# Gated linear attention before a mixture of experts: holding every second sequence with its chunk halves exchanged, and leaving out the scores that the causal mask removes

## The chip, the cores and the metric

The kernel runs on one NeuronCore of a Trainium2 chip. The metric is the device time of one execution in microseconds (us). The engines are named as in the profile: PE is the matrix engine (PEld its weight loads), DVE the vector engine, ACT the scalar engine, POOL the GpSimd engine, and SP the engine that issues most of the DMAs.

## The reference, cut to what matters

An attention block with a decaying state feeds an expert layer with two levels of routing. There are 4 batches, 8 heads, 768 steps and a head size of 48; 3072 tokens of 384 features reach 16 experts with a hidden size of 1024.

```python
def _attn_ref(q, k, v, f_logit):                 # each (4, 8, 768, 48)
    f = 1.0 / (1.0 + np.exp(-f_logit))
    for t in range(S):
        state = f[:, :, t, :, None] * state + np.einsum('bhd,bhe->bhde', k[:, :, t], v[:, :, t])
        y[:, :, t] = np.einsum('bhd,bhde->bhe', q[:, :, t], state)

def _moe_ref(x, w_group, w_expert, w1, w2):      # x (3072, 384)
    # argmax of x @ w_group picks a group, argmax of xg @ w_expert[g] an expert in it
    h = np.maximum(xg[mask_e] @ w1[g, e], 0.0)
    out[tok_idx] = (g_w * e_w)[:, None] * (h @ w2[g, e])
```

## The kernel before

**The attention part** works on chunks of 128 steps. A unit is one chunk of two sequences (two batches, eight heads each), so there are 6 x 2 = 12 units, numbered 0 to 11; even and odd units are the two pairs of batches of the same chunk. In a unit the sequences are called b = 0 and 1, the eight heads are four pairs a with a member r = 0 or 1. A chunk's 128 steps lie on the 128 partitions as they come from memory; after a transpose the two heads of a pair lie on partitions 0 to 47 and 64 to 111.

A unit runs through stages, each a generator that issues a little of its work at each step:

- load (L568): four transfers on SP's queue, f, k, q and v, each of both sequences (f of unit 0 in two). k and q of unit i+2 and f of unit i+3 are asked for at the start of unit i.
- bounded, gated (L577, L584): the log gates, their cumulative sum over the chunk as a matmul with the triangle `tri` (L600), and two exponentials of it. The last row of one exponential goes by a small DMA to `ends` (L607); `decayed` (L638) turns it into the decay of the chunk.
- multiplied, turned (L614, L626): q and k times those exponentials on DVE (L620, L623), then transposes (L634) copied by ACT to Tq and Tk (L635).
- scored (L647): for every head the 128 x 128 products of keys and queries, written as two matmuls, one for each half of the keys, with all 128 queries (L659). DVE multiplies them by `tri` (L662), which leaves queries at or after their key. The result is `am`, one tile for each sequence.
- stated (L665): keys times values (L676) for the state of the next chunk (`sp`, `st`, L682 and L683 on DVE).
- weighed (L688): in its first step the state times the queries (L697, from the second chunk on), in its second the values times `am` (L701), both summed in the same two PSUM banks; ACT copies them to xT (L704).
- done, listed (L707, L729): logits of the router (L717), and rows of x turned back (L742) and sent to memory.

PSUM is eight banks given out in turn under the name bank. Matmuls with 48 rows and 64 columns use one of four tiles of the array, those of 128 rows and 64 columns one of two. Every fp32 product appears in the trace as two pairs of a weight load and a matmul; the transposes appear as one.

**The order of the work** on PE, DVE, ACT and SP is written out by hand: BEGIN for units 0 to 2, EVEN and ODD for the others, ORDERS for the last. A letter with an offset names the stage and the unit. In EVEN "s s s s c+2 w d-1 g+2 w" means: scores of b = 0, their masks, scores of b = 1, their masks, then the state products, the router logits of the unit before, and the outputs. POOL's order is left to the scheduler.

**The routing** of a chunk (route, L178) runs step by step among the units, mainly on DVE. After chunk 3 two experts are picked early and their weights loaded; after the last chunk all are ranked. **The expert part** runs 16 passes of two matmuls each (up L432 and L439, down L465 with L460 or L475), with tokens gathered and results scattered by indirect DMAs of POOL (L393, L450). Two early passes fill PE while the last routing runs. Behind the passes stand a slower path for gates that decay too far (scan) and one for experts with more tokens than foreseen; both are skipped with these inputs.

Of the kernel before, what the change touches and what calls it, by code (L numbers as in the profile page):

```python
# [10 lines left out]
FP32 = mybir.dt.float32  # L11
# [4 lines left out]
OP = mybir.AluOpType  # L16
AX = mybir.AxisListType.X
ET = mybir.EngineType
P = 128
# [4 lines left out]
def kernel(  # L24
# [12 lines left out]
    nc = tc.nc  # L37
# [56 lines left out]
    halves = const([P, 2], FP32, "halves")  # L94
    make_upper_triangular(nc, tri, val=1.0, diag=True)
    make_identity(nc, ident)
    nc.vector.memset(onesb, 1.0)
    nc.vector.tensor_tensor(strictb, tri, ident, OP.subtract)

# [219 lines left out]

    def choose(sb):  # L320
        number = numbers(sb)
        mine = sb.tile([P, 2, HP, P], FP32, tag="am", bufs=3, name="mine").rearrange("p r a t -> p (r a t)")[:, 0:2 * GE * GE].rearrange("p (n j e) -> p n j e", j=2, e=GE)
# [196 lines left out]
    with ExitStack() as fast:  # L519
# [44 lines left out]
        def parts(i):  # L564

            return (slice(0, 1), slice(1, 2)) if i == 0 else (slice(0, 2),)

        def load(i, names):  # L568
            c, s = units[i]
            w = live.setdefault(i, {"v": pads["v"][i % 4], "qh": pads["qh"][i % 3]})  # L570
            for nm in names:
                if nm not in w:
                    w[nm] = sb.tile([P, 2, H, D], FP32, tag="ld_" + nm, bufs=3 if nm == "f" else 2, name="ld_" + nm)
                for b in parts(i) if nm == "f" else (slice(0, 2),):
                    nc.sync.dma_start(out=heads(w[nm][:, b])[:, :, 0:D], in_=SRC[nm][2 * s + b.start:2 * s + b.stop, :, c * P:(c + 1) * P, :].rearrange("b h t d -> t (b h) d"))

        def bounded(i):  # L577

# [5 lines left out]
        def gated(i):  # L584

            c, s = units[i]
            w = live[i]

            nl = w["f"].rearrange("p b h d -> p b (h d)")
            for b in parts(i):  # L590
                nc.scalar.activation(nl[:, b], nl[:, b], AF.Exp, bias=0.0, scale=-1.0)
                if i:
                    yield
                nc.scalar.activation(nl[:, b], nl[:, b], AF.Ln, bias=1.0, scale=1.0)
            eq, qh, kh = pads["eq"][i % 2], w["qh"], pads["kh"][i % 3]
            w.update(eq=eq, kh=kh)
            yield
            for b in range(2):
                cs = bank([P, H, D], "cs")
                nc.tensor.matmul(cs.rearrange("t h d -> t (h d)"), lhsT=tri, rhs=nl[:, b], start=True, stop=True)  # L600
                nc.scalar.activation(eq[:, b, :, 0:D], cs, AF.Exp, bias=0.0, scale=-1.0)  # L601
                nc.scalar.activation(kh[:, b, :, 0:D], cs, AF.Exp, bias=0.0, scale=1.0)
                if b:

                    if s == 0:
                        ends[c] = sb.tile([B * HP, P], FP32, tag="ends", bufs=1, name="ends")
# [40 lines left out]
        def scored(i):  # L647
            w = live[i]
            w["am"] = []
            for b in range(2):  # L650
                am = sb.tile([P, 2, HP, P], FP32, tag="am", bufs=3, name="am")
                w["am"].append(am)
                ap = [bank([P, HP, P], f"ap{r}") for r in range(2)]
                for a in range(HP):
                    for r in range(2):
                        rows = slice(DP * r, DP * r + D)
                        for u in range(2):
                            half = slice(u * P // 2, (u + 1) * P // 2)
                            nc.tensor.matmul(ap[r][half, a, :], lhsT=w["Tk"][rows, b, a, half], rhs=w["Tq"][rows, b, a, :], start=True, stop=True)  # L659
                yield  # L660
                for r in range(2):
                    nc.vector.tensor_tensor(am[:, r], ap[r], tri.unsqueeze(1).broadcast_to((P, HP, P)), OP.mult)  # L662
                yield

        def stated(i):  # L665
# [22 lines left out]
        def weighed(i):  # L688
# [7 lines left out]
                        rows = slice(DP * (b ^ h), DP * (b ^ h) + D)  # L696
                        nc.tensor.matmul(ys[b][DP * h:DP * h + DP, a, :], lhsT=states[s][c % 2][rows, b, a, :], rhs=w["Tq"][rows, b, a, :], start=(a == 0), stop=False, skip_group_check=True)  # L697
            yield
            for b in range(2):
                for a, h in [(a, h) for a in range(HP) for h in range(2)]:  # L700
                    nc.tensor.matmul(ys[b][DP * h:DP * h + DP, a, :], lhsT=w["v"][:, b, 2 * a + (b ^ h), :], rhs=w["am"][b][:, b ^ h, a, :], start=(c == 0 and a == 0), stop=True, skip_group_check=True)  # L701
# [77 lines left out]
        def advance(gens):  # L779
# [8 lines left out]
        STAGES = {"c": bounded, "g": gated, "m": multiplied, "t": turned, "s": scored, "n": stated, "w": weighed, "d": done, "x": listed, "b": decayed}  # L788
        BEGIN = """c0 g0 p g0 g0 m0 m0 m0 m0 l2 t0 t0 t0 t0 h c1 g1 g1 s0 s0 s0 s0 g1 g1 p w0 w0 n0 m1 m1 m1 m1 l3 h x0 x0 x0
            t1 t1 t1 t1 b1 c2 g2 g2 s1 s1 s1 s1 p d0 g2 g2 n0 n1 w1 w1 m2 m2 l4 n1  # L790
            d0 x1 x1 t2 t2 t2 t2 c3 g3 g3 x1 s2 s2 s2 s2 w2 g3 g3 d1 w2 n2 m3 m3 c4 g4 g4""".split()
        BEGUN = 3
        EVEN = "l+2 d-2 n-1 r r r x-1 x-1 t t t t g+1 g+1 x-1 r s s s s c+2 w d-1 g+2 w g+2 n m+1 m+1".split()
        ODD = "l+2 d-2 r r x-1 x-1 t t t t b n-1 g+1 g+1 x-1 r s s s s c+2 w d-1 g+2 w g+2 n m+1 m+1 r n".split()
        ORDERS = {
            NU - 3: "l+2 o d-2 r r x-1 x-1 t t t t b n-1 r g+1 g+1 x-1 r s s s s c+2 w d-1 g+2 w g+2 n m+1 m+1 r n".split(),
            NU - 2: "d-2 r x-1 x-1 r t t t t r g+1 g+1 x-1 s s s s w d-1 w n m+1 m+1".split(),
            NU - 1: "d-2 r r n-1 x-1 x-1 t t t t r x-1 r s s s s w b d-1 w r r".split(),
            NU: "d-2 r e d-1 x-1 x-1 d-1 x-1 r r r e e r e r r e r r e r e r r e e e e e".split(),
        }  # L800
        steps_of = {}
# [144 lines left out]
    def scan():  # L946
# [42 lines left out]
        for c in range(NC):  # L989
            lgs = sb.tile([P, B, NL], FP32, tag="lgs2", name="lgs2")  # L990
            for b in range(B):
                x = sb.tile([P, HP, 2, DP], FP32, tag="x2", name="x2")
                nc.vector.memset(x, 0.0)
                for r in range(2):
                    nc.sync.dma_start(out=x[:, :, r, 0:D], in_=y_dram[b * HP:(b + 1) * HP, c * P:(c + 1) * P, r * D:(r + 1) * D].rearrange("a t d -> t a d"))
# [72 lines left out]
```

## Time and profile before

| What | Value |
|---|---|
| Median of 14 runs | 422.36 us (420.86 to 423.38) |
| Profiled execution | 421.6 us, of which the span is 419.7 us |
| PE busy | 408.8 us (97%), 4047 matmuls |
| PEld busy | 376.4 us (90%) |
| DVE, ACT, POOL busy | 266.8, 156.8 and 83.0 us |
| Scores L659 | 24.4 us on PE, x768 |
| Outputs L701 | 24.4 us on PE, x384 |
| State products L697, keys times values L676 | 10.7 and 11.0 us, x320 each |
| Masks L662 | 29.8 us on DVE, x48 |
| Attention part | to about 137 us of the span, then the expert passes |
| Mean granted clock of PE | 0.993 |

A busy figure counts the time in which at least one instruction of the group ran, so matmuls that lie side by side in the array count once; the mean of one is much longer than its share. A line of the form "start, length, what" in the chain of waits is a stretch of the work that ended last, in order of time; "x64" is the number of instructions in it. In the timeline, a bracket gives the idle time before the first of a group and what ended it.

### The profile page before, as it was taken

To read this page: it belongs to the slowest core of one execution; us is meant where nothing else is said; L and a number is where in the kernel's file an instruction comes from. 1 tells how busy PE (TensorE), PEld (TensorE's weight loads), DVE (VectorE), ACT (ScalarE), POOL (GpSimd) and SP (SyncE) were. 2 spreads that over 40 slices of the span, in tenths; PEclk is the share of its full clock that TensorE was granted. 3 is DMA by queue.
4 is the path that set the end of the run, shared out by engine and by line. 5 is a ranking of instruction groups with operands and counts; after the bars stand their busy time and mean duration, and the time that the engine had idled before them with its cause. 6 is when DMAs were issued, how large, how long until landed. Compare 5 with 4: busy or idle time off the path is not lost.

```text
span 419.7 us, 10066 instructions
## 1 busy us (share of the span) xinstructions
PE 408.8 (97%) x4047; PEld 376.4 (90%) x4047; DVE 266.8 (64%) x778; ACT 156.8 (37%) x353; POOL 83.0 (20%) x127
## 2 busy tenths in 40 slices
PE   7999999999999998999999999999999999999995
PEld 3888888888878966879999999999999999999992
DVE  5666878878897810550599786495595595594240
ACT  6777776667554311111123122231231231231220
POOL 4000010101012166001031321312222221120230
PEclk9999999999999999899999999999999999999998
DMA  9999997878999369937548485595695795585010
GB/s 176 197 202 215 188 179 152 155 141 157 334 340 387 110 242 340 372 120 278 177 154 291 121 313 199 199 328 134 249 318 141 276 301 197 216 319 161 27 46 24
DMA packets 132145, 88.98 MB, mean 212 GB/s; under 512 B 102582, under 2 KB 122748, under 8 KB 132090
## 3 DMA queue, kind: packets, MB, share of 16 engines
q1 hardware_dynamic: 125666, 75.50, 61.4%
q0 software_dynamic: 5792, 11.92, 9.4%
q10 hardware_dynamic: 632, 0.83, 0.6%
q8 instruction: 34, 0.56, 0.6%
q14 instruction: 21, 0.17, 0.1%
HBM read 78.71 MB, written 9.83 MB: 211 GB/s over the span
## 4 chain that ended last, share of the span: by engine, by line
PE 48%; issue 29%; DMA 8%; POOL 6%; DVE 4%; another core or an unknown queue 2%; POOLq 1%; ACT 1%; SPq 0%; DVEq 0%
PE hp L439 11%; DMA out_dram<-yt,xg 6%; PE yo L475 6%; PE ap L659 5%; PE y L701 5%; POOL out_dram L450 4%; PE cs L600 3%; PE yo L460 3%; PE x_ps L742 2%; POOL xg L393 2%; PE tr_k L634 2%; PE ds L676 2%; PE y L697 2%; PE tr_q L634 2%
## 5 line engine op out<-in xcount | busy, mean ns | idle before, releaser
L439 PE MATMUL hp<-xe,w 128*128 128x128 f32 (+14 forms) x864 | 141.7, 323 | 2.2 <-issue 1.5
L439 PEld LDWEIGHTS hp<-xe,w 128*128 128x128 f32 x864 | 137.5, 192 | 4.4 <-issue 2.4
L475 PE MATMUL yo<-h,w 128*128 128x230 f32 (+13 forms) x672 | 115.8, 333 | 0.0
L422 DVE STREAM_TRANSPOSE yr<-yT 32x192 f32<-32x192 f32 (+1 forms) x208 | 70.5, 339 | 70.5 <-ACT yT L476 67.9
L475 PEld LDWEIGHTS yo<-h,w 128*128 128x128 f32 x672 | 113.7, 190 | 0.2
L415 DVE STREAM_TRANSPOSE xe<-xg 32x192 f32<-32x192 f32 (+1 forms) x208 | 69.7, 335 | 8.7 <-PE hp L439 5.7
L440 ACT ACTIVATE h<-hp 128x256 f32<-128x256 f32 (+14 forms) x72 | 34.2, 478 | 109.1 <-PE hp L439 102.3
L450 POOL DMA_INDIRECT out_dram<-yt,xg x32 | 34.4, 1076 | 155.5 <-ACT yt L447 150.0
L476 ACT COPY yT<-yo 128x230 f32<-128x230 f32 (+13 forms) x42 | 13.5, 325 | 80.5 <-PE yo L475 80.5
L393 POOL DMA_INDIRECT xg<-x_dram,rows_p x30 | 29.6, 986 | 51.7 <-DMA out_dram<-yt,xg 29.1
L662 DVE TENSOR_TENSOR am<-ap,tri 128x512 f32<-128x512 f32 x48 | 29.8, 682 | 12.0 <-PE ap L659 12.0
L659 PE MATMUL ap<-Tq,Tk 48*64 48x128 f32 x768 | 24.4, 273 | 0.5 <-issue 0.5
L701 PE MATMUL y<-am,v 128*64 128x128 f32 x384 | 24.4, 276 | 0.2
L701 PEld LDWEIGHTS y<-am,v 128*64 128x64 f32 x384 | 20.9, 137 | 3.3 <-issue 1.8
L659 PEld LDWEIGHTS ap<-Tq,Tk 48*64 48x64 f32 x768 | 21.0, 133 | 2.5 <-issue 2.0
L460 PE MATMUL yo<-w,h 128*128 128x384 f32 x64 | 21.3, 486 | 0.0
L600 PE MATMUL cs<-ld_f,tri 128*128 128x384 f32 x48 | 18.6, 506 | 0.5 <-issue 0.4
L460 PEld LDWEIGHTS yo<-w,h 128*128 128x128 f32 x64 | 11.9, 190 | 7.4
L447 ACT ACTIVATE yt<-yr,xg 128x384 f32<-128x384 f32 (+13 forms) x26 | 14.4, 604 | 5.4 <-DVE yr L422 5.4
L607 POOL DMA_DIRECT2D ends<-eq x10 | 5.4, 541 | 55.7 <-ACT eq L601 55.7
L704 ACT COPY xT<-y 128x512 f32<-128x512 f32 x24 | 13.5, 580 | 4.4 <-PE y L701 4.3
L430 DVE COPY xe<-xg_ps 128x384 f32<-128x384 f32 (+1 forms) x4 | 2.1, 536 | 20.5 <-remote 9.6
(173 smaller groups left out, 381.9 us busy)
## 6 DMA issues: line engine op xcount, KB each, us to landing
w<-in_moe_w_dram SPq DMA_DIRECT2D x34, 1536.0 KB, 7.3
qh<-in_q_dram SPq DMA_DIRECT2D x12, 384.0 KB, 4.4
ld_k<-in_k_dram SPq DMA_DIRECT2D x12, 384.0 KB, 5.7
v<-in_v_dram SPq DMA_DIRECT2D x12, 384.0 KB, 7.6
ld_f<-in_f_logit_dram SPq DMA_DIRECT2D x11, 384.0 KB, 5.7
x_dram<-x_kept SPq DMA_DIRECT2D x2, 1536.0 KB
x_dram<-x POOLq DMA_DIRECT2D x2, 384.0 KB
x_dram<-x ACTq DMA_DIRECT2D x2, 384.0 KB
```

The source lines that it names most:

```text
L393: nc.gpsimd.indirect_dma_start(out=w["x"][:, j, :], out_offset=None, in_=x_dram[0:1 + top, :], in_offset=bass.IndirectOffsetOnAxis(ap=rows ...
L415: squares(w, lambda n, k_, rk, g, rg: nc.vector.transpose(out=xT[rg, 0:n, k_], in_=x[rk, 0:n, g]))
L422: squares(w, lambda n, k_, rk, g, rg: nc.vector.transpose(out=y[rk, 0:n, g], in_=yT[rg, 0:n, k_]))
L439: nc.tensor.matmul(hp[:, o, :], lhsT=w1[:, ko, (f + o) * P:(f + o + 1) * P], rhs=w["xT"][:, ko, :], start=(ko == 0), stop=(ko == KO - 1))
L440: nc.scalar.activation(h[:, f:f + 2, :], hp, AF.Relu)
L450: sent = nc.gpsimd.indirect_dma_start(out=out, out_offset=bass.IndirectOffsetOnAxis(ap=w["x"][0:m, j, DM + 1:RW].bitcast(U32), axis=0), in ...
L460: nc.tensor.matmul(yp, lhsT=w["h"][:, fo, :], rhs=w2[:, fo, :], start=(fo == 0), stop=(fo == FO - 1))
L475: nc.tensor.matmul(yp, lhsT=w2[:, fo, m * P:(m + 1) * P], rhs=w["h"][:, fo, :], start=(fo == 0), stop=(fo == FO - 1))
L600: nc.tensor.matmul(cs.rearrange("t h d -> t (h d)"), lhsT=tri, rhs=nl[:, b], start=True, stop=True)
L659: nc.tensor.matmul(ap[r][half, a, :], lhsT=w["Tk"][rows, b, a, half], rhs=w["Tq"][rows, b, a, :], start=True, stop=True)
L662: nc.vector.tensor_tensor(am[:, r], ap[r], tri.unsqueeze(1).broadcast_to((P, HP, P)), OP.mult)
L701: nc.tensor.matmul(ys[b][DP * h:DP * h + DP, a, :], lhsT=w["v"][:, b, 2 * a + (b ^ h), :], rhs=w["am"][b][:, b ^ h, a, :], start=(c == 0 a ...
```

## The change

For the second sequence of a unit (b = 1) the two halves of a chunk are exchanged on the partitions: steps 64 to 127 lie on partitions 0 to 63 (E), steps 0 to 63 on 64 to 127 (L). Every load is therefore three transfers: the first sequence whole, the second in two halves. The cumulative sum of b = 1 uses another triangle, `swapped`, and its chunk end is row 63 instead of 127, so `ends` takes two transfers a unit. Token numbers of odd batches are exchanged alike.

Keys of a chunk's later half are no longer multiplied with queries of its earlier half. The scores of one head of both sequences lie in 192 columns of 128 partitions instead of 256: early keys with all 128 queries, late keys with the 64 late queries. A score tile holds two head pairs of both sequences instead of four of one, and its mask is `seen`, three blocks of 64 columns. The outputs of late queries are summed over all 128 keys, those of early queries over the 64 early keys alone, with 64 columns for each matmul. In the written orders the first step of w moves between the two halves of the scores, "s s s s ... w" to "s s w s s", from unit 2 on. The path that is skipped (scan) and choose are adapted.

```diff
+    HF = P // 2
+    E, L = slice(0, HF), slice(HF, P)
+    swapped = const([P, P], FP32, "swapped")
+    seen = const([P, 3, HF], FP32, "seen")
+    nc.gpsimd.tensor_copy(swapped, tri)
+    nc.gpsimd.memset(swapped[E, L], 0.0)
+    nc.gpsimd.memset(swapped[L, E], 1.0)
+    nc.gpsimd.tensor_copy(seen[:, 0, :], swapped[:, E])
+    for rows in (E, L):
+        nc.gpsimd.tensor_copy(seen[rows, 1, :], tri[rows, rows])
+    nc.gpsimd.tensor_copy(seen[:, 2, :], tri[:, L])
+    sums = (tri, swapped)
...
+        swap = token.rearrange("p c (s b) -> p c s b", b=2)[:, :, :, 1]
+        nc.vector.tensor_scalar(swap, swap, HF, None, OP.bitwise_xor)
...
-                for b in parts(i) if nm == "f" else (slice(0, 2),):
-                    nc.sync.dma_start(out=heads(w[nm][:, b])[:, :, 0:D], in_=SRC[nm][2 * s + b.start:2 * s + b.stop, :, c * P:(c + 1) * P, :].rearrange("b h t d -> t (b h) d"))
+                for b, rows, at in ((0, slice(0, P), 0), (1, E, HF), (1, L, 0)):
+                    first = c * P + at
+                    nc.sync.dma_start(out=w[nm][rows, b, :, 0:D], in_=SRC[nm][2 * s + b, :, first:first + rows.stop - rows.start, :].rearrange("h t d -> t h d"))
...
-                nc.tensor.matmul(cs.rearrange("t h d -> t (h d)"), lhsT=tri, rhs=nl[:, b], start=True, stop=True)
+                nc.tensor.matmul(cs.rearrange("t h d -> t (h d)"), lhsT=sums[b], rhs=nl[:, b], start=True, stop=True)
...
-                if b:
...
-                    side(i).dma_start(out=ends[c][2 * HP * s:2 * HP * (s + 1), :], in_=eq[P - 1:P].rearrange("o b (a r) d -> o (b a) (r d)", r=2))
+                end, to = (HF if b else P) - 1, (2 * s + b) * HP
+                side(i).dma_start(out=ends[c][to:to + HP, :], in_=eq[end:end + 1, b].rearrange("o (a r) d -> o a (r d)", r=2))
...
-            for b in range(2):
-                am = sb.tile([P, 2, HP, P], FP32, tag="am", bufs=3, name="am")
+            for m in range(HP // 2):
+                am = sb.tile([P, 2, 2, 3 * HF], FP32, tag="am", bufs=3, name="am")
                 w["am"].append(am)
-                ap = [bank([P, HP, P], f"ap{r}") for r in range(2)]
-                for a in range(HP):
-                    for r in range(2):
-                        rows = slice(DP * r, DP * r + D)
-                        for u in range(2):
-                            half = slice(u * P // 2, (u + 1) * P // 2)
-                            nc.tensor.matmul(ap[r][half, a, :], lhsT=w["Tk"][rows, b, a, half], rhs=w["Tq"][rows, b, a, :], start=True, stop=True)
+                ap = [bank([P, 2, 3 * HF], f"ap{r}") for r in range(2)]
+                for j in range(2):
+                    for early in (True, False):
+                        for r in range(2):
+                            rows = slice(DP * r, DP * r + D)
+                            for b in range(2):
+                                keys, to = (E, L) if early else (L, E), HF * (b if early else 1 - b)
+                                mine = keys[b]
+                                asked = slice(0, P) if early else mine
+                                at = HF * (1 - b) if early else 2 * HF * (1 - b)
+                                nc.tensor.matmul(ap[r][to:to + HF, j, at:at + asked.stop - asked.start], lhsT=w["Tk"][rows, b, 2 * m + j, mine], rhs=w["Tq"][rows, b, 2 * m + j, asked], start=True, stop=True)
                 yield
                 for r in range(2):
-                    nc.vector.tensor_tensor(am[:, r], ap[r], tri.unsqueeze(1).broadcast_to((P, HP, P)), OP.mult)
+                    nc.vector.tensor_tensor(am[:, r], ap[r], seen.rearrange("p n t -> p (n t)").unsqueeze(1).broadcast_to((P, 2, 3 * HF)), OP.mult)
...
-            for b in range(2):
-                for a, h in [(a, h) for a in range(HP) for h in range(2)]:
-                    nc.tensor.matmul(ys[b][DP * h:DP * h + DP, a, :], lhsT=w["v"][:, b, 2 * a + (b ^ h), :], rhs=w["am"][b][:, b ^ h, a, :], start=(c == 0 and a == 0), stop=True, skip_group_check=True)
+            for early in (False, True):
+                for a in range(HP):
+                    for h in range(2):
+                        for b in range(2):
+                            mine, other = ((E, L), (L, E))[b]
+                            rows, asked = (mine, mine) if early else (slice(0, P), other)
+                            at = HF if early else 2 * HF * (1 - b)
+                            nc.tensor.matmul(ys[b][DP * h:DP * h + DP, a, asked], lhsT=w["v"][rows, b, 2 * a + (b ^ h), :], rhs=w["am"][a // 2][rows, b ^ h, a % 2, at:at + HF], start=(c == 0 and a == 0 and not early), stop=True, skip_group_check=True)
...
-        EVEN = "l+2 d-2 n-1 r r r x-1 x-1 t t t t g+1 g+1 x-1 r s s s s c+2 w d-1 g+2 w g+2 n m+1 m+1".split()
+        EVEN = "l+2 d-2 n-1 r r r x-1 x-1 t t t t g+1 g+1 x-1 r s s w s s c+2 d-1 g+2 w g+2 n m+1 m+1".split()
```

ODD, the orders of the last units and unit 2 in BEGIN change in the same way.

More of the change, by code (lines that the diff above doesn't have):

```diff
@@ L321, in choose @@
         number = numbers(sb)
-        mine = sb.tile([P, 2, HP, P], FP32, tag="am", bufs=3, name="mine").rearrange("p r a t -> p (r a t)")[:, 0:2 * GE * GE].rearrange("p (n j e) -> p n j e", j=2, e=GE)
+        mine = sb.tile([P, 2, 2, 3 * HF], FP32, tag="am", bufs=3, name="mine").rearrange("p r a t -> p (r a t)")[:, 0:2 * GE * GE].rearrange("p (n j e) -> p n j e", j=2, e=GE)
         got = sb.tile([P, GE, 2], FP32, tag="got", bufs=1, name="got")
@@ L599, in gated @@
                 cs = bank([P, H, D], "cs")
-                nc.tensor.matmul(cs.rearrange("t h d -> t (h d)"), lhsT=tri, rhs=nl[:, b], start=True, stop=True)
+                nc.tensor.matmul(cs.rearrange("t h d -> t (h d)"), lhsT=sums[b], rhs=nl[:, b], start=True, stop=True)
                 nc.scalar.activation(eq[:, b, :, 0:D], cs, AF.Exp, bias=0.0, scale=-1.0)
                 nc.scalar.activation(kh[:, b, :, 0:D], cs, AF.Exp, bias=0.0, scale=1.0)
-                if b:
-                    if s == 0:
-                        ends[c] = sb.tile([B * HP, P], FP32, tag="ends", bufs=1, name="ends")
-                    side(i).dma_start(out=ends[c][2 * HP * s:2 * HP * (s + 1), :], in_=eq[P - 1:P].rearrange("o b (a r) d -> o (b a) (r d)", r=2))
+                if s == 0 and b == 0:
+                    ends[c] = sb.tile([B * HP, P], FP32, tag="ends", bufs=1, name="ends")
+                end, to = (HF if b else P) - 1, (2 * s + b) * HP
+                side(i).dma_start(out=ends[c][to:to + HP, :], in_=eq[end:end + 1, b].rearrange("o (a r) d -> o a (r d)", r=2))
                 yield
@@ L790 @@
             t1 t1 t1 t1 b1 c2 g2 g2 s1 s1 s1 s1 p d0 g2 g2 n0 n1 w1 w1 m2 m2 l4 n1
-            d0 x1 x1 t2 t2 t2 t2 c3 g3 g3 x1 s2 s2 s2 s2 w2 g3 g3 d1 w2 n2 m3 m3 c4 g4 g4""".split()
+            d0 x1 x1 t2 t2 t2 t2 c3 g3 g3 x1 s2 s2 w2 s2 s2 g3 g3 d1 w2 n2 m3 m3 c4 g4 g4""".split()
         BEGUN = 3
-        EVEN = "l+2 d-2 n-1 r r r x-1 x-1 t t t t g+1 g+1 x-1 r s s s s c+2 w d-1 g+2 w g+2 n m+1 m+1".split()
-        ODD = "l+2 d-2 r r x-1 x-1 t t t t b n-1 g+1 g+1 x-1 r s s s s c+2 w d-1 g+2 w g+2 n m+1 m+1 r n".split()
+        EVEN = "l+2 d-2 n-1 r r r x-1 x-1 t t t t g+1 g+1 x-1 r s s w s s c+2 d-1 g+2 w g+2 n m+1 m+1".split()
+        ODD = "l+2 d-2 r r x-1 x-1 t t t t b n-1 g+1 g+1 x-1 r s s w s s c+2 d-1 g+2 w g+2 n m+1 m+1 r n".split()
         ORDERS = {
-            NU - 3: "l+2 o d-2 r r x-1 x-1 t t t t b n-1 r g+1 g+1 x-1 r s s s s c+2 w d-1 g+2 w g+2 n m+1 m+1 r n".split(),
-            NU - 2: "d-2 r x-1 x-1 r t t t t r g+1 g+1 x-1 s s s s w d-1 w n m+1 m+1".split(),
-            NU - 1: "d-2 r r n-1 x-1 x-1 t t t t r x-1 r s s s s w b d-1 w r r".split(),
+            NU - 3: "l+2 o d-2 r r x-1 x-1 t t t t b n-1 r g+1 g+1 x-1 r s s w s s c+2 d-1 g+2 w g+2 n m+1 m+1 r n".split(),
+            NU - 2: "d-2 r x-1 x-1 r t t t t r g+1 g+1 x-1 s s w s s d-1 w n m+1 m+1".split(),
+            NU - 1: "d-2 r r n-1 x-1 x-1 t t t t r x-1 r s s w s s b d-1 w r r".split(),
             NU: "d-2 r e d-1 x-1 x-1 d-1 x-1 r r r e e r e r r e r r e r e r r e e e e e".split(),
@@ L994, in scan @@
                 for r in range(2):
-                    nc.sync.dma_start(out=x[:, :, r, 0:D], in_=y_dram[b * HP:(b + 1) * HP, c * P:(c + 1) * P, r * D:(r + 1) * D].rearrange("a t d -> t a d"))
+                    for rows in (E, L):
+                        first = c * P + (rows.start ^ HF if b % 2 else rows.start)
+                        nc.sync.dma_start(out=x[rows, :, r, 0:D], in_=y_dram[b * HP:(b + 1) * HP, first:first + HF, r * D:(r + 1) * D].rearrange("a t d -> t a d"))
                 xr = sb.tile([P, HP, 2, D], FP32, tag="x2r", name="x2r")
```

## The prediction

> **What bounds the kernel now.** The page's slices come first, then the chain of waits, the timeline around one unit, the groups with their shapes, and the DMA issues on SP.
>
> ```profile
> PE   7999999999999998999999999999999999999995
> DVE  5666878878897810550599786495595595594240
> ...
> DMA  9999997878999369937548485595695795585010
> ```
>
> One slice is 10.5 us. The attention part is slices 1 to 13; there PE is never under 9 tenths, DVE runs at 7 to 8 and the DMA engines at 9 in the first six. So PE is the suspect, and the chain has to confirm it:
>
> ```profile
> 41.20 1.49 PE cs L600 x4
> ...
> 42.81 1.91 PE ap L659 x64
> 44.72 0.87 PE y L697 x32
> 45.59 0.57 PE lT L717 x16
> 46.16 1.90 PE y L701 x32
> 48.06 0.92 PE ds L676 x32
> ...
> 102.39 0.45 PE x_ps L742 x4
> 102.86 0.48 ACT x L744
> ...
> 109.88 1.86 DVE am L662 x3
> ...
> 179.69 5.16 PE yo L460 x16
> ```
>
> From 20 to 102 us the chain is PE after PE, one unit in 10.4 us; each piece begins where the last ended. Units 2 to 8 therefore give every saved PE us to the end. In unit 9 (103 to 117) DVE and ACT carry it, in units 10 and 11 mostly PE again. Behind that the expert passes follow in order from the routing, so I let a shorter attention part move them whole; a stand of 5 us at 162 to 167, where PE, ACT and DVE wait on nothing that the profile names, I leave as it is.
>
> "x64" counts pairs of a weight load and its matmul; one fp32 product is two pairs (32 products a unit, 12 units, x768). Tiles of the array work side by side: L697 fills four tiles (48 rows by 64 columns), L676 and L701 two (128 by 64). Per round, one pair on each tile, L697 needs 0.87/8 = 0.109 us at 128 columns, L701 0.109 also, and L676 0.92/16 = 0.0575 at 48 columns. The wide L460 gives 5.16/16/384 = 0.84 ns a column, so 128 columns should cost 0.108 (they do) and 48 should cost 0.040 (they do not): below some 68 columns a round costs 0.0575, set by its weight loads. Where the tile size changes, a piece has a surplus: L717 0.57 - 4 x 0.109 = 0.13, L701 1.90 - 16 x 0.109 = 0.16, L659 1.91 - 16 x 0.109 = 0.17; L697, of L659's size, has none. I call that a switch, 0.15 us.
>
> Do four tiles load weights side by side too? The timeline of the first 0.1 us of L659, and then DVE's masks:
>
> ```profile
> 42.74 0.21 PEld L659 LDWEIGHTS ap<-Tq,Tk 48*64 48x64 f32 x8
> ...
> 43.88 2.48 DVE L662 TENSOR_TENSOR am<-ap,tri 128x512 f32<-128x512 f32 x4 [0.94 <-PE ap L659]
> ```
>
> Eight loads, two a tile, start within 0.1 us and end in 0.21 with 0.13 for a single one: they do.
>
> **Scores (L659).** As many pairs as before, but half of the 16 rounds have 64 columns instead of 128. Streaming 64 columns takes 64 x 0.84 = 54 ns, so the weight loads' 0.0575 decides. Saved: 8 x (0.109 - 0.0575) = 0.41 us a unit. The four tiles stay distinct: r is the row half, and the two sequences take opposite column halves.
>
> **Outputs (L701).** 16 products of 128 columns become 16 full-depth ones of 64 (two tiles, 16 rounds) and 16 half-depth ones of 64 (four tiles, 8 rounds): 24 x 0.0575 = 1.38 instead of 16 x 0.109 = 1.74, saving 0.36. But the tile size changes twice more, between the two loops and before L676, which follows without a switch now: 2 x 0.15. Net -0.06. The full-depth loop names the same column half twice in a row (h outside, b inside). L659's program does that too, two pairs of one product and then the next tile, and runs four tiles abreast, so I charge nothing; if it ran a column half at a time, at most 16 x 0.0575 = 0.9 us more.
>
> **Masks (L662).** Their shape is then that of L682:
>
> ```profile
> L662 DVE TENSOR_TENSOR am<-ap,tri 128x512 f32<-128x512 f32 x48 | 29.8, 682 | 12.0 <-PE ap L659 12.0
> ...
> L682 DVE TENSOR_TENSOR sp<-st,ds 128x384 f32<-128x384 f32 x8 | 4.4, 547 | 0.0
> ```
>
> 48 x 0.135 = 6.5 us of DVE, on the path in unit 9 alone: 4 x 0.135 = 0.54 there. DVE waits for PE ahead of the masks, so elsewhere it is worth nothing.
>
> **Order ("s s w s s").** The state products (L697) go between the halves of the scores. They need st (L683), in the tightest units ready between 0.3 us before and 0.2 us after the scores' start, while L697 comes 0.7 after it: no wait. But PE now reaches the outputs sooner than the second mask pair is ready. From the scores' start: first half 0.72, L697 to 1.59, second half to 2.26, its masks from 2.47 (0.21 behind PE, as in the timeline) to 3.5; outputs start at 2.26 + 0.15 + 0.44 + 0.15 = 3.0 and need the second pair after eight rounds, at 3.45. A new wait on DVE am of about 0.15 us (0 to 0.3); queued behind it are the outputs, ACT's xT copies and L676.
>
> So a unit saves 0.41 + 0.06 - 0.15 = 0.32 us. Units 0 and 1 have no L697 and some idle PE between transposes, and the wait does not arise: 0.3 each.
>
> **Loads.** Each of 48 loads (49 issues) becomes three issues: all of the first sequence, then two half-partition transfers. SP's timeline and the one DVE wait on them late enough to matter:
>
> ```profile
> 10.24 1.48 SPq L575 DMA_DIRECT2D ld_k<-in_k_dram  x1
> ...
> 59.05 0.37 SPq L575 DMA_DIRECT2D ld_k<-in_k_dram  x1
> 59.52 1.95 SPq L575 DMA_DIRECT2D qh<-in_q_dram  x1
> ```
>
> ```profile
> 17.27 0.56 DVE L623 SCALAR_TENSOR_TENSOR kh<-kh,ld_k 128x384 f32<-128x384 f32 x1 [1.04 <-DMA ld_k<-in_k_dram]
> ```
>
> Until 55 us SP issues back to back, 1.3 to 2.9 us each; later an issue that finds the queue empty takes 0.37. So most of an issue now is waiting for the queue to drain, and bytes and packets stay. If the added issues only share that drain they are free; if each adds its own 0.37, eight a unit add 3.0 us to the 7.6 us that four loads take, about the 10.4 us pitch. The start is tight either way: unit 0 begins with SP issues and a 5.92 us k landing on the chain, and unit 1 has about 1 us of cover. On the other side the first sequence's k can be used before the second's has landed. I take +0.5 us (-0.3 to +2). The Trainium skill, page "DMA: Bandwidth & Descriptors", section "Rules for kernel authors", speaks against the split: transfers to disjoint partition halves serialize, use one of 128 partitions. By it the halves bring nothing and cost only their issue, which is what my bound already holds.
>
> **Waits and small work.** Readers of a loaded tile may wait on three semaphores for one; a semaphore instruction on PE lasts 51 ns in L701's rows. 12 x 0.05 = 0.6 us on PE (0 to 0.6). The second ends transfer a unit costs POOL 0.54 (10 of them, POOL idles 55.7 us ahead of L607) and ACT 0.7 twice (ACT idles 2.4 us before the next lgT): hidden. Eight set-up instructions on POOL at 0.1 to 0.3 us, at most 2 us, push it from 4.1 to 6.1; the first swapped sum is wanted at 6.5 and the DVE exchange of token numbers far later: nothing. Were that cover gone, up to 0.5 us at the start.
>
> **Sum.** 7 x 0.32 + 0.54 + 2 x 0.32 + 2 x 0.3 = 4.0 us saved, less 0.6 and 0.5: 2.9. The profiled execution took 421.6 us (span 419.7 and 1.9 around it), giving 418.7; the median of the runs is 0.76 above it, so 419.5. Without the am wait and the semaphores, and with 0.3 gained at the start: 11 x 0.47 + 0.54 + 0.3 = 6.0, or 416.4.
>
> **Rivals.** First, slower: pairs cannot follow each other faster than the trace has ever shown. The quickest sustained row is L697, 0.87/32 = 27 ns a pair; my four-tile rounds of 64 columns want 14.4. Held to 27, the scores save nothing and the outputs cost 0.16 + 0.92 + 0.15 + 0.87 + 0.15 = 2.25 against 1.90: +0.35 a unit, 11 units, less unit 9's 0.2, plus 0.6 and 0.5: +4.7, 427.1. It decides from about 19 ns a pair, where 64 pairs x 5 ns eat the 0.32 of a unit. For it: no row is faster. Against it: eight loads started in 0.1 us above, and the four members of a round stand together. The Trainium skill, page "TensorE: Matmul & The Clock Gate", section "Wait — 56ns, not 53.3ns?", states that matmul starts never come closer than about 25 ns however few the columns. By that the case would come out near an estimated +0.21 a unit, but eight starts in 0.1 us do not fit it.
>
> Second, the loads become the bound in the first 55 us: it begins where an added issue costs over 0.08 us (unit 1's 1 us of cover against 13 added issues up to its k). At the full 0.37 it is 13 x 0.37 - 1 = 3.8 us there in place of my 0.5, and up to 4 more where units 2 and 3 lose theirs: 4.0 - 0.6 - 3.8 = 0.4 slower at least, 422.8 to 427. At a third of that price, 0.6, it is my own case. For it: DMA at 9 tenths and SP never idle. Against it: the 0.37 issue, and waiting as most of the rest.
>
> Third, no difference: the PE time comes free but the next wait takes it, DVE or ACT (71 and 67 us busy of the 93 from 11 to 104), so that a unit saves under 0.15: 421.6 to 423.2.
>
> **How the numbers follow.** The main case gets 0.60 (0.04 of it within 0.2%), the pair floor 0.16 (0.01 within), the loads 0.14 (0.02 within), the swallowed gain 0.10 (0.07 within, 0.03 slower). That is faster 0.56, same 0.14, slower 0.30; 0.2%, 0.8 us, is what a measurement of this kernel can tell from no change. The range starts at 416.4 and reaches to 425.5, taking in most of the loads' case and the pair floor up to +3.1; the main case alone is 416.4 to 421.5.
>
> **What would show it.** L659 still x768, in the chain about 0.67 us for x32 on either side of L697; L701 x768 at some 1.7 us a unit with a gap inside it; a wait on DVE am in L701 near 0.15 us a unit; L676 with 0.15 before it; L662 near 547 ns; the first chain piece still a k landing near 8.7 us. A new L659 still at 1.7 to 1.9 us for both halves proves the pair floor, and DVE waits on ld_k, ld_f or v after 20 us the loads. Units at 10.4 us pitch or more would make the prediction wrong.

## The result, and the profile after

The changed kernel is slower. Its median is 435.45 us (433.55 to 436.63, 10 runs) beside 422.34 us for the kernel before; the ratio is 1.031 (95% interval 1.029 to 1.033), 13 us where 2.9 us less were predicted, and outside the predicted range. The kernel before took 416.4 to 422.3 us on the chips used below, so every ratio is one against the kernel before on the same chip.

The page's slices of the profiled execution (span 431.1 us, a slice is 10.8 us):

```profile
PE   7999999999997599799999999999999999999994
...
PEclk9999999999999699999999999999999999999998
DMA  8988788878799938987384684865865876685110
```

PE has a hole in slices 13 and 14, where the attention part ends and where it was full before the change; its granted clock drops in slice 14; and the DMA engines are *less* busy in the first slices than before the change (8 and 7 where there were 9s). Next the chain of waits:

```profile
45.76 4.78 DMA ld_f<-in_f_logit_dram
...
57.76 4.55 DMA ld_f<-in_f_logit_dram
...
79.24 0.83 PE ap L680 x32
80.07 0.88 PE y L718 x32
80.94 0.67 PE ap L680 x32
81.61 0.57 PE lT L743 x16
82.19 1.85 PE y L727 x63
84.04 1.10 PE ds L697 x32
...
138.42 6.95 DMA xg<-x_dram,rows_e
```

The unit in the middle is what was predicted: two halves of scores (0.83 holds the switch, 0.67 does not), outputs in 1.85 us. Around it the chain now goes through loads of f, and at 138 us through the gather of the first early expert pass. SP's timeline tells why that gather is late. Before the change:

```profile
105.27 3.88 SPq L758 DMA_DIRECT2D x_dram<-x_kept  x2
```

and after it:

```profile
122.33 2.66 SPq L784 DMA_DIRECT2D x_dram<-x_kept  x2
127.59 38.25 SPq L397 DMA_DIRECT2D w<-in_moe_w_dram  x7
```

The kept rows of units 0 to 7 and the early experts' weights stand behind the loads on SP, which ended by 105 us and now end at 122. The second send of kept rows landed at 137.4 us (120.7 before), one microsecond ahead of the gather that reads them:

```profile
138.42 1.07 POOL L409 DMA_INDIRECT xg<-x_dram,rows_e  x1 [14.40 <-DVE val L249]
```

Before the change:

```profile
126.90 1.07 POOL L393 DMA_INDIRECT xg<-x_dram,rows_e  x1 [6.94 <-DVE low L302]
```

(The releaser in brackets is an inference; after the change the landing of the send is the later event. Before the change the last rows to land ahead of the gather were those that POOL sends itself, at 125.5.) So the lateness is made in two places, read from the starts of the scores and of the first expert matmul: unit 5 starts at 69.0 instead of 64.0, which is 5.0 us; from there to unit 9 the change even gains a little (111.3 - 69.0 = 42.3 against 106.7 - 64.0 = 42.7); the first expert matmul starts at 149.5 instead of 136.8, 12.7 late, so about 8 more are lost behind unit 9. The end of the span is 11.3 later.

### The profile page after: what moved, and what is told of

It reads as the page before. It is cut to its first block, busy times and chain, and to the rows that moved or that the text cites. A ratio compares the mean times of both kernels' runs of the same rounds, so it can differ in the third digit from the quotient of the medians.

```text
span 431.1 us, 11074 instructions
## 1 busy us (share of the span) xinstructions
PE 407.3 (94%) x4431; PEld 373.7 (87%) x4431; DVE 261.8 (61%) x779; ACT 156.7 (36%) x353; POOL 90.2 (21%) x144
## 4 chain that ended last, share of the span: by engine, by line
PE 39%; issue 29%; DMA 11%; ACT 6%; POOL 6%; DVE 2%; another core or an unknown queue 2%; SPq 2%; POOLq 1%; ACTq 0%; DVEq 0%
PE hp L455 11%; DMA out_dram<-yt,xg 7%; PE yo L491 6%; PE y L727 4%; POOL out_dram L466 3%; PE ap L680 3%; PE yo L476 3%; DMA ld_f<-in_f_logit_dram 3%; PE cs L617 3%; POOL xg L409 2%; SPq L592 2%; PE x_ps L768 2%; PE y L718 2%; PE ds L697 2%
## 5 line engine op out<-in xcount | busy, mean ns | idle before, releaser
L455 PE MATMUL hp<-xe,w 128*128 128x128 f32 (+14 forms) x864 | 139.4, 320 | 2.8 <-issue 2.0
L455 PEld LDWEIGHTS hp<-xe,w 128*128 128x128 f32 x864 | 136.1, 190 | 4.1 <-issue 1.7
L683 DVE TENSOR_TENSOR am<-ap,seen 128x384 f32<-128x384 f32 x48 | 24.2, 551 | 13.1 <-PE ap L680 13.1
L727 PEld LDWEIGHTS y<-am,v 128*64 128x64 f32 (+1 forms) x768 | 21.7, 140 | 7.2 <-issue 4.6
L727 PE MATMUL y<-am,v 128*64 128x64 f32 (+1 forms) x768 | 24.7, 232 | 3.2 <-issue 2.7
L623 POOL DMA_DIRECT2D ends<-eq x20 | 10.7, 533 | 74.8 <-ACT eq L618 74.7
L680 PE MATMUL ap<-Tq,Tk 48*64 48x128 f32 (+1 forms) x768 | 22.2, 247 | 1.2 <-ACT Tk L651 1.2
L680 PEld LDWEIGHTS ap<-Tq,Tk 48*64 48x64 f32 x768 | 19.5, 133 | 3.5 <-ACT Tk L651 2.1
L768 PE MATMUL x_ps<-ident,xT 128*128 128x128 f32 x96 | 13.6, 288 | 1.9 <-ACT xT L730 1.9
L608 ACT ACTIVATE ld_f<-ld_f 128x768 f32<-128x768 f32 (+1 forms) x13 | 10.4, 804 | 12.9 <-DVE ld_f L598 12.9
```

The costliest lines, as they stand in the source:

```text
L455: nc.tensor.matmul(hp[:, o, :], lhsT=w1[:, ko, (f + o) * P:(f + o + 1) * P], rhs=w["xT"][:, ko, :], start=(ko == 0), stop=(ko == KO - 1))
L680: nc.tensor.matmul(ap[r][to:to + HF, j, at:at + asked.stop - asked.start], lhsT=w["Tk"][rows, b, 2 * m + j, mine], rhs=w["Tq"][rows, b, 2 ...
L683: nc.vector.tensor_tensor(am[:, r], ap[r], seen.rearrange("p n t -> p (n t)").unsqueeze(1).broadcast_to((P, 2, 3 * HF)), OP.mult)
L727: nc.tensor.matmul(ys[b][DP * h:DP * h + DP, a, asked], lhsT=w["v"][rows, b, 2 * a + (b ^ h), :], rhs=w["am"][a // 2][rows, b ^ h, a % 2, ...
L768: nc.tensor.transpose(out=pt[:, a].rearrange("t h d -> t (h d)"), in_=xT[:, b, a, :], identity=ident)
```

## The experiments

The first theory was that the number of issues on SP costs the time; its rival was that the products, masks and order do. All readings that follow are gathered here: the ratio to before, the start of unit 5's scores and that of the first expert matmul, in us.

| Kernel | Ratio (95% interval) | Unit 5 | First expert |
|---|---|---|---|
| before | 1 | 64.0 | 136.8 |
| changed | 1.031 (1.029 to 1.033) | 69.0 | 149.5 |
| e1 three issues, halves of partitions | 1.026 (1.023 to 1.029) | 67.6 | 148.9 |
| e2 two issues | 1.001 (0.999 to 1.003) | 63.8 | 137.3 |
| e6 three issues, by heads | 1.002 (1.000 to 1.005) | 63.8 | 136.8 |
| e3 new products, second v loaded | 1.024 (1.022 to 1.026) | 66.6 | 147.7 |
| e5 new products, second v copied by POOL | 1.018 (1.013 to 1.022) | 64.5 | 142.0 |
| e9 outputs cut in two | 1.014 (1.010 to 1.018) | 64.9 | 143.3 |
| e11 e1 and e9 together | 1.026 (1.023 to 1.029) | 67.8 | 149.4 |
| e4 changed, kept rows sent by POOL | 1.037 (1.031 to 1.044) | 76.8 | 157.0 |
| e7 changed, kept rows sent early | 1.020 (1.016 to 1.025) | 67.1 | 146.7 |
| e8 scores alone | 0.999 (0.996 to 1.001) | 65.6 | 138.3 |
| e10 scores alone, copies moved | 0.999 (0.998 to 1.000) | 64.5 | 136.7 |
| e12 e10, order of the end edited | 0.999 (0.997 to 1.000) | 64.8 | 137.0 |
| e13 before, order of the end edited | 0.999 (0.998 to 1.001) | 64.1 | 137.3 |
| e14 e12, outputs by sequence | 1.004 (1.002 to 1.006) | 64.6 | 137.2 |

The starts come from one profiled execution each, on several chips. In e2, e6 and e13, which cost nothing, they differ from those of the kernel before by up to 0.2 and 0.5 us; smaller differences say nothing.

**e1_three and e2_two: the loads by themselves, in the kernel before.**

```
-  for b in parts(i) if nm == "f" else (slice(0, 2),): ...
+  for b, rows in ((0, slice(0, P)), (1, slice(0, P // 2)), (1, slice(P // 2, P))):      # e1
+      nc.sync.dma_start(out=w[nm][rows, b, :, 0:D], ...)
+  for b in range(2):                                                                     # e2
+      nc.sync.dma_start(out=w[nm][:, b, :, 0:D], ...)
```

> The kernel before with only its loads changed: each of f, k, q and v of a unit in three issues (first sequence whole, second sequence in two partition halves, at their natural places), 12 issues a unit as after the change, and none of its products, masks or order. Theory 1, the number of issues on SP is the cause (after the change an issue that stands directly behind another took about 0.6 us and some 0.05 to the next, 12 x 0.65 = 7.8 us a unit, and the sends of the kept rows and the expert weights queue behind them): this kernel has all of the loss and none of the saving on PE, so slower than before by 10 to 17 us, 432 to 439, with DVE waits on ld_f in the first 60 us and the weights issued 10 us or more later. Theory 2, the new products, masks and order cost the time and the loads are hidden: 421 to 424.

> The kernel before with each load in two issues, one a sequence, both of 128 partitions: 8 issues a unit in place of 4, no halves. If the number of issues alone counts at about 0.65 us each (theory 1), 8 x 0.65 = 5.2 us a unit is still less than the 7.6 us that the bytes took before, so little is lost: 422 to 425. If it is the halves of partitions that cost and not the count, also 422 to 424, so it tells the count from the halves only together with the three-issue kernel: a loss here of a third or more of that kernel's loss speaks for the count. Theory 2 (products and order): 421 to 424.

e1 has none of the new products and still loses 11.3 us of 416.5, with the first expert matmul 12.1 us late. The loads alone make most of the loss (1.026 of 1.031). Eight whole-width issues a unit cost nothing.

**e6_heads: count or halves?** The same 12 issues of the same sizes, the second sequence cut by heads, so that all transfers write 128 partitions.

```
+  for b, hs in ((0, slice(0, H)), (1, slice(0, H // 2)), (1, slice(H // 2, H))):
+      nc.sync.dma_start(out=w[nm][:, b, hs, 0:D], ...)
```

> The kernel before with each load in three issues as in the three-issue kernel, 12 a unit and of the same sizes, but the second sequence is cut by heads (0 to 3 and 4 to 7) and not by halves of partitions, so that every transfer writes 128 partitions. If the number of issues is what slows the loads: again slower by 8 to 13 us (ratio 1.02 to 1.03). If it is the transfers of 64 partitions: like the two-issue kernel, ratio 1.00 to 1.005.

It is the transfers of 64 partitions: 12 issues cost 0.002, or nothing. So the first theory, the count of issues, falls. The DMA queues from 10 to 55 us (packets, MB, share of the 16 engines), before, e6, e1 and changed:

```profile
q1 hardware_dynamic: 47186, 8.99, 103.1%
```

```profile
q1 hardware_dynamic: 43184, 8.10, 93.4%
```

```profile
q1 hardware_dynamic: 38690, 7.26, 85.7%
```

```profile
q1 hardware_dynamic: 37880, 7.11, 84.9%
```

The engines move less while SP issues without a pause (in e1 never over 0.44 us between two loads up to 55 us). An issue of 96 KB to 64 partitions never takes under 0.60 us (median 0.633, 96 of them in e1), one of the same 96 KB to 128 partitions at least 0.457 (median 0.568, 96 in e6); and up to 55 us the first kind lands on average about 0.66 us after the transfer before it, the second 0.49. With eight a unit, 8 x 0.17 = 1.4 us. Five units' packets had started after 40.7 us before the change, 44.4 in e6, 49.1 in e1, 48.3 changed; less the 1.8 us at which the first starts, that is 7.8, 8.5, 9.5 and 9.3 us a unit. So of the 1.7 us by which a unit's loads are slower in e1, 0.7 come with the count (and cost nothing in the end) and 1.0 with the width. At a unit pitch of 10.4 us the first two run ahead until the buffers are full: between 55 and 105 us SP then stands four times for about 5 us before the change, and for 1.3 and 3.3 us in e6. In e1 and the changed kernel it never stands for over 0.2 us there. The packets of the last unit had started after 110.5, 110.8, 124.3 and 124.9 us. The Trainium skill, page "DMA: Bandwidth & Descriptors", section "Rules for kernel authors", says that transfers to disjoint partition halves serialize and that one of 128 partitions should be used. The advice held: the halves are no faster together and each pays more than a cut by heads; why a half's issue is dearer no run here shows.

**e3_v_only and e5_v_pool: the new products with the loads as before.** f, k and q stay in place; only the outputs' v of the odd sequence is needed on exchanged partitions, as a second copy `vt`, loaded in e3 and copied on the chip in e5.

```
+  seen = const([P, 3, HF], FP32, "seen")      # mask of 192 columns, keys in natural order
+  nc.gpsimd.tensor_copy(w["vt"][rows, :, 0:D], w["v"][other, 1, :, 0:D])      # e5, in multiplied
```

> The new scores, outputs, masks and order, but f, k and q loaded as before, in one issue each at their natural places; only v of the odd sequence gets a second, exchanged copy by two half loads, because the outputs need it on the other partitions. 6 issues a unit in place of 12, an eighth more bytes. Theory 1: the saving on PE (0.3 us a unit as predicted, some 3 us in all) shows, less up to 1 us for the added v: 418.5 to 421.5, faster than both. Theory 2: the products and the order are the loss and it stays near the changed kernel, 428 or more; not below 422 in any case.

> The new scores, outputs, masks and order with the loads exactly as before the change (four issues a unit, natural places); the exchanged copy of the odd sequence's v is made on the chip by two POOL copies a unit instead of by loads. If the loads are the whole of the loss, what stays is the saving on PE, predicted as 0.3 us a unit, less some am wait: faster than before by 2 to 5 us, a ratio of 0.988 to 0.995, with no idle time of PE marked issue beyond 0.5 us before 146 us. If the products and the order cost time too: 1.00 or more.

In neither does the hoped-for saving show. e3 adds two half transfers a unit and an eighth more bytes and loses 10.2 us, so it can't tell the two apart. e5 adds no byte and no issue and still loses 7 us of 421.6; there is a second cause in the products. The chain of e5 names it:

```profile
115.89 1.77 issue
...
123.24 2.08 issue
...
136.54 1.69 issue
```

PE stands at these places with nothing to wait for that the profile knows; with 0.59 at 80 us they make 6.1 us, and the first expert matmul is 5.2 late. Counted through PE's records in the trace (weight loads, matmuls and semaphores), these stalls fall on numbers 3266, 4802, 5058 and 5570, all multiples of 256 apart. In e3 five such records have stalls, of 0.62, 1.42, 2.75, 0.73 and 2.04 us. The page's instruction queue moves 0.61 MB in 37 packets, 16 KB each. In e5 such a packet ended at 116.35 and PE went on at 117.67; 124.02 and 125.32; 136.87 and 138.23. So PE waits for the next block of its own program, until 1.3 us past that block's landing; and the packet of these three began only 3.3 to 5.4 us after PE had crossed into the block before, with loads and weights on the DMA engines.

**e9_split: more instructions and nothing else.** The kernel before, each output product cut in two of 64 columns: as many added weight loads and matmuls as in the change (768 each).

```
+  for q_ in range(2):
+      half = slice(q_ * P // 2, (q_ + 1) * P // 2)
+      nc.tensor.matmul(ys[b][..., a, half], lhsT=w["v"][...], rhs=w["am"][b][:, b ^ h, a, half], ...)
```

> The kernel before with each of its 16 output products a unit cut into two of 64 columns: 768 more weight loads and matmuls, as many as the change adds, and nothing else. The streams alone should cost 32 rounds of 0.0575 us against 16 of 0.109: 0.1 us a unit, 1.2 us in all, ratio 1.003. If late blocks of PE's program are a cost of more and shorter instructions, there are stalls of 1 to 3 us marked issue at every 256th instruction between 110 and 146 us besides, and the ratio is 1.008 to 1.017.

Confirmed: 1.014, 6 us, of which the chain shows 12 x 0.15 = 1.8 in longer outputs and three stalls, at records 4802, 5058 and 5570, of 0.92, 0.79 and 2.21 us:

```profile
117.88 0.11 PE tr_q L634
117.99 0.92 issue
...
136.04 2.21 issue
138.26 0.74 PE y L703 x17
```

The page's instruction queue has 37 packets (0.61 MB) where it had 34 (0.56 MB). Three more blocks are little; what counts is that a block is used up before the next one comes, and short pairs use it up sooner. They are not the only way to it: e1 and e2, which have the old pairs, each have one such stall, 3.24 and 1.40 us at record 4802, where the kernel before has none. The Trainium skill, page "Runtime: NRT & Kernel Launch", section "Instruction fetch mechanics", gives the blocks of 16 KiB (256 instructions) and calls the cost of crossing one mostly hidden. The size agrees with the records; the cost does not always: here up to 2.2 us a crossing in e9 and 3.24 in e1.

**e11_both: do the two add?**

> The kernel before with both suspects and none of the change's products: loads in three issues with two halves of partitions (alone 1.0259) and each output product cut into two of 64 columns (768 more instructions on PE, alone 1.0139). If the two losses are independent they add: 1.040, some 17 us. If they meet in the same place (both come out at the end of the attention part, where the loads, kept rows and weights hold the DMA engines), 1.028 to 1.035. The changed kernel had 1.031 with a saving of some 3 us on PE in it, so 1.038 is what it would take to account for all of it.

They do not add: 1.026, as e1 alone. Both end in the same wait, PE standing for the early gather (issued at 136.91 in e11, 137.55 in e1), so a stall ahead of it is free (e1 has one too, the 3.24 us above). The changed kernel is at the same place (first expert matmul at 149.5, 149.4 and 148.9; its own stall of 2.35 us at record 5570 lies ahead of 4.25 us of waiting for the gather). Its ratio is 0.005 above e11's, on another chip; that 2 us is not assigned.

**e4_kept_pool and e7_kept_early: the tail.** In e4 the kept rows go out from POOL's queue, in e7 from SP's but earlier.

```
-  nc.sync.dma_start(out=rows_of(2 * j, 0, 2 * B)[:, :, 0:DM], in_=t)
+  nc.gpsimd.dma_start(...)                                        # e4
-  NU - 3: "l+2 o d-2 ..."
+  5: ["o"] + ODD, NU - 3: "o l+2 d-2 ..."                         # e7, each "o" sends the newest group
```

> The changed kernel with one edit: the kept rows are sent to x_dram from POOL's queue in place of SP's, so that they no longer stand behind the loads. Theory 1 with the tail by way of the kept rows (sent by SP at 122.3 us after the change, 105.3 before; the early gather of x_dram is issued 11.5 us later): the early gather comes up to 8 us sooner and the kernel loses most of the part behind 115 us, 427 to 431. If the tail comes from the weights behind the same loads, or from the routing itself, it stays at 434 to 436.

> The changed kernel with the kept rows of units 0 to 3 sent at step 5 and those of units 4 to 7 ahead of the last unit's loads, where the changed kernel sends both behind them (its second send landed at 137.4 us and the early gather started at 138.4). If the tail hangs on that send, the gather starts near 130 us and the first expert pass 5 to 8 us sooner: ratio to before 1.010 to 1.022 where the changed kernel had 1.031. If the tail hangs on the DMA engines being full (the weights then land as late, and PE's program too), 1.025 to 1.035.

e4 was a miss, 1.037 (1.031 to 1.044) with times scattered from 428.9 to 436.9: its profiled execution, the longest of its four, is 12.7 us late at unit 5 (76.8). A stall of 2.67 us at record 2242 is in that; the rest this run does not separate, so it settles nothing. In e7 the second send landed at 123.2 and the gather came 9 us sooner:

```profile
129.38 1.35 POOL L409 DMA_INDIRECT xg<-x_dram,rows_e  x1 [3.38 <-DMA qh<-in_q_dram]
```

The ratio went from 1.031 to 1.020, in the upper half of what the first reading expected. So the tail does hang on that send. Not all of it: the weights still came at 130.5 and an f load still held unit 7 (92.2, where the changed kernel had 89.7), and ACT stood 4.10 us ahead of unit 10's copies for something that the profile does not name. In the profiled execution the first expert matmul was only 2.8 us sooner.

**e8_scores and e10_scores2: what the scores alone bring.** Loads, order, 128-column outputs and instruction count as before, the outputs of the two sequences taken in turn; the exchange of the odd sequence is made by two POOL copies of v, and by an exchanged identity in the transposes of its q. e10 moves the copies from `multiplied` to `scored`.

```
+  identity=exchange if nm == "q" and b else ident
+  nc.tensor.matmul(out_, lhsT=w["Tk"][..., E if early else L], rhs=w["Tq"][..., slice(0, P) if early else late], ...)
```

> Only the scores of the change: four-tile products of 128 and of 64 columns, no more instructions on PE than before; loads and order as before, outputs again 16 products of 128 columns, masks again 512 columns (the shared block of early queries is read twice and zeroed for the other sequence's keys). The odd sequence's v is exchanged by two POOL copies and its queries by an exchanged identity in their transposes. If what the exchanged-copy kernel lost (1.0175) is the 10 per cent more PE instructions, whose program blocks arrive late, this kernel shows the saving of the scores, 0.4 us a unit: 3 to 5 us, ratio 0.988 to 0.994, with under 1 us of PE idle marked issue. If the 64-column scores, the POOL copies or the exchanged v cost the time, 1.00 or more.

> The scores-only kernel with its two POOL copies moved from the step of the gates' products to the first step of the scores, so that POOL no longer waits for the load of v ahead of the next send of the chunk ends (in the scores-only kernel that chain, v 6.8 us, copies 1.5, ends 3.5, held unit 3 back by 1.9 us). If that is what ate the saving: unit 3 starts within 0.3 us of before, units at 10.2 to 10.3 us pitch instead of 10.6, and 2.5 to 4.5 us gained: ratio 0.990 to 0.994. If the saving is swallowed at the early gather (7 us in flight) or in unit 9 anyway: 0.995 to 1.00.

No stalls of PE's program any more, and each unit's scores are 0.41 us shorter:

```profile
85.33 1.50 PE ap L684 x64
```

e8 was a miss all the same, 0.999. It lost 1.9 us at unit 3, because POOL stood for v ahead of the next send of `ends`; e10 lost only 0.9 there and was 1.0 ahead at unit 9 (105.7 against 106.7; e2, e6 and e13, with the old scores, had 106.4, 106.4 and 107.1). But the ratio of e10 is 0.999 (0.998 to 1.000). PE's timeline shows where the rest went:

```profile
134.13 0.52 PE L443 MATMUL xg_ps<-ident,xg 128*128 128x128 f32 x3 [1.38 <-DMA xg<-x_dram,rows_e]
```

The gather (issued at 126.75, 7.25 us in flight) lands when it landed before, and PE stands 1.4 us for it with the last unit's logits queued behind.

**e12_order, e13_order_before, e14_turns: can the saving be had?** e12 puts these transposes behind the last unit's logits, e13 does so in the kernel before, e14 also computes the outputs one sequence after the other again, as before the change.

```
-  NU: "d-2 r e d-1 x-1 x-1 d-1 x-1 r r r e e ..."
+  NU: "d-2 r d-1 x-1 x-1 d-1 x-1 e r r r e e ..."      # e12, e13, e14
-  for a in range(HP): for b, h in CORNERS: ...
+  for b in range(2): for a, h in ...: ...              # e14
```

> The scores-only kernel with its copies moved, and one edit to the written order: in the step behind the last unit, the transposes of the early gather (PE, in order) stand behind the router logits and the row transposes of unit 11 and no longer ahead of them. In the kernel without this edit PE stood 1.4 us for the gather at 132.8 us with unit 11's logits queued behind it, and the scores' gain (1.0 us at unit 9, 1.4 with unit 11's outputs) was gone at 134. If the gather's flight is what swallows the saving, the router's last ranking comes 1.2 to 2 us sooner and the kernel gains 1.0 to 2.0 us on the kernel before: ratio 0.995 to 0.998. If something behind it (the pass itself, its weights) is the bound: 0.998 to 1.001.

> The control: the kernel before with the same edit of the order alone. Its gather lands as PE reaches the transposes, so there is hardly a wait to be had: ratio 0.998 to 1.001. If it gains as much as the kernel above, the edit and not the scores is the gain.

> The kernel of the run with the edited order, with the outputs again one sequence after the other (b outside, as before the change) in place of both in turn. In the run with both in turn ACT could begin its two copies to xT only when all outputs were done (1.08 us in one piece ahead of unit 11's logits, 0.59 in the control), and in units 1 and 2, where ACT carries the chain, unit 3 started 0.9 us later than before. If that ate the rest of the saving, 0.5 to 2 us more than the run before it: ratio to before 0.994 to 0.9975. If the second pair of masks, now wanted 0.44 us sooner, or the early pass holds the end, 0.998 to 1.000.

e12: 0.999 (0.997 to 1.000); e13: 0.999 (0.998 to 1.001). The wait for the gather is gone, yet the first expert matmul starts at 137.0 and 137.3; ACT's copies of x and of the gathered rows carry the chain there instead. e14: 1.004 (1.002 to 1.006), a miss. Its chain shows DVE taking the place of PE in units 3, 7 and 9, here in unit 7:

```profile
85.63 0.84 PE ap L684 x31
86.50 0.77 DVE am L687 x2
...
87.71 1.28 DVE am L687 x2
...
89.45 0.87 DVE qh L637
90.32 1.20 DVE kh L640
```

The chain of e12 has the same places, and unit 8 besides. So they tell where the shorter scores are lost, and not why e14 is slower than e12; that stays open. No version here beats the kernel before by more than can be measured.

## Why the prediction was wrong, point by point

**The step that failed is "Loads".** I took +0.5 us (-0.3 to +2), from the price of an issue on an empty queue (0.37) and the thought that added issues share the drain. The count was indeed free (e6). The width was not: the eight 64-partition transfers a unit cost about 0.17 us each in pace against transfers of the same bytes to 128, and the loads lost the lead that they had over the units (e1: 11.3 us alone). The remark that the halves "bring nothing and cost only their issue" was the mistake in words: I priced a half by the row of a 128-partition issue. The +2 at its end is not a fifth of that.

**The rival for the loads was right in kind and stopped too early.** It gave 3.8 us in unit 1 and up to 4 more; measured were 1.6 at unit 1 and 5.0 at unit 5. It did not follow SP's queue on: the kept rows and the weights are issued from it behind the last load. This is the second failed step, "the expert passes move whole": they start with a gather that waits for the kept rows, and the other 8 us are lost around it (2.35 in a stall ahead of the wait, 4.25 in the wait, 1.5 at half the clock behind it). With the kept rows sent earlier, e7 had a ratio of 1.020 in place of 1.031.

**A term was missing: PE's program.** I counted the 32 added pairs a unit of the outputs as time on the array only. As instructions, 768 more weight loads and matmuls, they cost 6 us by themselves (e9), 1.8 of it on the array and the rest by late blocks of the program. In the changed kernel that loss is mostly hidden behind the gather (e11).

**What held.** Scores: 0.83 + 0.67 = 1.50 against 1.91, the 0.41 of the forecast. Outputs and the step behind them: 1.85 + 1.10 = 2.95 against 1.90 + 0.92 = 2.82, so +0.13 where -0.06 and 0.15 of waiting gave +0.09; the switch ahead of the state's products, which had none, is their 1.10 less 0.92, 0.18. Masks: 

```profile
L683 DVE TENSOR_TENSOR am<-ap,seen 128x384 f32<-128x384 f32 x48 | 24.2, 551 | 13.1 <-PE ap L680 13.1
```

551 ns where 547 was taken. Semaphores: up to 140 us PE's records hold 120 of them where there were 73, so 47 more and not the 12 of the forecast; e6 has 42 more at a ratio of 1.002, so they cost little. Four units of e5 took 107.1 - 64.5 = 42.6 us, less the stall of 0.59 in them, against 42.7: 0.17 a unit saved where 0.32 was worked out; DVE held one of the four (unit 7). One reading was loose, though nothing rests on it: in slices 1 to 13 DVE runs at 5 to 9 tenths and not at 7 to 8, and PE is at 7 in the first.

**The pair floor is refuted.** In the trace of the changed kernel the four-tile rounds of L727 start 58 ns apart (in unit 6 at 1335, 1393, 1451 and 1510 ns from the first matmul), four matmuls each: 14.6 ns a pair, as the forecast wanted. The Trainium skill's 25 ns between matmul starts (page "TensorE: Matmul & The Clock Gate", section "Wait — 56ns, not 53.3ns?") does not hold across four tiles; the measurement decides.

**The third rival, a gain that the next wait takes,** is what became of the scores once nothing else was in their way (e10, e12, e14), in part by DVE and ACT, as it said, and in e10 at the end by the early gather, which it did not name.

## What to carry to other kernels

When a load is cut, price the new shape and not the count, and compare the pace at which the loads then run with the pitch of the work: a lead that no longer builds up is lost behind the last load, so read on down the issuing queue to whatever stands there. Count instructions as well as cycles: where pairs become shorter and more, the engine's program is one more stream that has to arrive in time; here it came late mostly between 111 and 143 us, where kept rows and weights were moved. (That they delay it is not shown.) A stage that is shortened is worth what the next wait lets through; in e10 that was a gather in flight for 7 us, and in e12, with it out of the way, ACT's copies.

## What the runs showed of the hardware that was not expected

An issue on SP that writes 64 partitions took at least 0.60 us, one of the same bytes over 128 partitions 0.457. PE's program comes in blocks of 256 instructions, and where PE stood for one it went on 1.2 to 1.5 us after the block's packet had ended, so that crossing into one could cost up to 3.24 us (e1). After some idle times of PE its granted clock was 0.5 for a while: 3.4 us from 86.7 in e7, behind 2.1 us without a matmul, and 10.2 us from 138.5 in the changed kernel, behind 2.35 us; behind 2.08 us in e5 it was not. This is a part of the 8 us in the changed kernel: the gathered rows' transposes, the last logits and the last rows took 0.88, 1.01 and 1.68 us behind the gather where they took 0.33, 0.74 and 1.03 before the change, 1.5 us more beside 2.35 of stall and 4.25 of waiting. In e7 four transposes took twice their 0.44 us:

```profile
87.46 0.85 PE tr_q L650 x4
```

An exchanged identity in the transposes gave the exchanged halves of a chunk at the price of the plain one (0.44 us for four in e10, the same as before).
